# The first three loads of SyncE in another order, in a fused attention and feed-forward kernel

## Chip, cores and metric

The kernel runs on one core of a Trainium2 chip. The metric is the time of one execution in microseconds (us), measured on the device; the number given for a kernel is the median of its runs. The engines are named as in the profile: PE (TensorE matmuls), PEld (its weight loads), DVE (VectorE), ACT (ScalarE), POOL (GpSimd) and SP (SyncE), the last two of which here mainly issue DMAs.

## What is computed

Linear attention over 8 batches, 8 heads, 1024 positions and a head size of 64, followed by a feed-forward layer with a maximum of two branches. All inputs and outputs are float32.

```python
k_proj = einsum('ks,bhsd->bhkd', E, k)          # E: 64 x 1024
v_proj = einsum('ks,bhsd->bhkd', F, v)          # F: 64 x 1024
attn   = softmax(q @ k_proj^T / 8)              # over the 64 projected positions
x      = (attn @ v_proj), heads side by side    # 8192 x 512
out    = maximum(x @ w1, x @ w2) @ w_out        # 512 -> 1024 -> 512
```

## The kernel before, in words

Matmuls run in float16 with float32 sums. Loads of k, q, v and the weights go through POOL's DMA queue, which casts float32 to float16 on the way. The work is a list of steps by batch, written out by hand: each engine's instructions come in the order in which the program's steps are called. Batch 0 has a beginning of its own, which the change touches; from about 23 us on come the products of the feed-forward layer, with the attention of the next batch laid in between.

The beginning of batch 0, with the lines of the profile:

- SP issues three loads that aren't cast (L86 to L88): E into the first half of `ef_sb` (64 partitions of 4 KB, 256 KB), heads 0 and 1 of batch 0's k into `kf_sb` (128 partitions, two runs of 2 KB each, 512 KB), and F into the second half of `ef_sb` (256 KB). `ef_sb` lies in the buffer that the profile calls `big`; `kf_sb` uses the room of the later weight `wo_sb`.
- POOL issues, in its own queue (L108), heads 2 and 3 of k, heads 0 to 3 of q, 4 to 7 of k, 4 to 7 of q, then v in four loads of two heads each, then the weights (L130, L139, L143).
- DVE fills a tile with ones. PE runs eight matmuls on it (`warm(8)`, L153), whose results nobody reads; more such fillers stand between the later steps.
- `step_eft(0)`: PE turns E in eight float32 transposes (L167) and DVE casts the result to float16 (L173). `step_eft(1)` does so for F, with ACT casting.
- DVE casts head 0 of `kf_sb` (L959), ACT head 1 (L960).
- `warm(5)`, then `step_kv(t, 0, 4, "k")`: the product of E and heads 0 to 3 of k (L195). It needs the cast E, both casts of `kf_sb` and POOL's first load.
- `step_eft(1)`, then `step_kpt` (L285, L290) turns the projected k; `step_qt` (L311, L316) turns q; `step_sc` gives scores (L340) and exponentials on ACT (L380); `step_dn` the sums over the projected positions (L352) and their logarithm (L388); `step_inv` the reciprocal (L427). The same follows for heads 4 to 7.
- `step_kv(..., "v")` (L195) projects v with the turned F as its loads come in; `step_at` (L352, L443) forms the attention's output; the feed-forward products begin at L524.

The order on SP alone is what the change touches. Nothing in the program ties one of the three loads to another; what waits for them are the instructions that read their tiles: L167 for E and for F, L959 and L960 for `kf_sb`.

Of the kernel before, what the change touches and what calls it, by code (L numbers as in the profile page):

```python
# [19 lines left out]
def kernel(  # L20
# [12 lines left out]
    nc = tc.nc  # L33
# [5 lines left out]
    NC = S // 128  # L39
# [25 lines left out]
    def mm_bank(dtype=FP32, n=None):  # L65
        if n is None:
            n = turn.pop(0)
            turn.append(n)
        return ps.tile([128, 512 if dtype == FP32 else 1024], dtype, tag=f"mm{n}", name="mm_ps")
# [9 lines left out]
    def big(n, dtype=FP16):  # L79
# [3 lines left out]
    kf_sb = const.tile([128, 2048], FP32, tag="wo", name="kf_sb")[:, 0 : 2 * NC * D].rearrange(  # L83
        "p (h c d) -> p h c d", h=2, d=D
    )
    nc.sync.dma_start(out=ef_sb[:, 0, :], in_=E)  # L86
    nc.sync.dma_start(out=kf_sb, in_=k[0, 0:2].rearrange("h (p c) d -> p h c d", c=NC))
    nc.sync.dma_start(out=ef_sb[:, 1, :], in_=F)  # L88
    nc.scalar.add_instruction(
        mybir.InstLoadActFuncSet(  # L90
# [37 lines left out]
    for g in range(2):  # L128
        for w_sb, w in ((w2_sb, moe_w2), (w1_sb, moe_w1)):
            nc.gpsimd.dma_start(  # L130
                out=w_sb.rearrange("p (g z) f -> p g z f", z=2)[:, g, :, 0:256],
                in_=w.rearrange("(g p z) f -> p g z f", p=128, z=2)[:, g, :, 0:256],
            )
    for w_sb, w, f0, f1 in (
# [3 lines left out]
        for z in range(2):  # L138
            nc.gpsimd.dma_start(  # L139
                out=w_sb.rearrange("p (g z) f -> p g z f", z=2)[:, :, z, f0:f1],  # L140
                in_=w.rearrange("(g p z) f -> p g z f", p=128, z=2)[:, :, z, f0:f1],
# [994 lines left out]
    for i, (new, old) in enumerate(zip([*groups[1:], none], groups)):  # L1136
        n, h = divmod(i + 2, 2)
# [54 lines left out]
    for reg in regs:  # L1192
# [4 lines left out]
        out=mm_bank()[0:1, 0:1], lhsT=ones16[:, 0:1], rhs=ones16[:, 0:1], start=True, stop=True  # L1197
# [166 lines left out]
```

## Time and profile before

| | us |
|---|---|
| median of 3 runs | 319.77 (319.64 to 320.38) |
| the profiled execution | 319.9 |
| its span in the profile | 318.1 |
| PE busy in the span | 312.3 (98%) |
| DVE, ACT, POOL busy | 241.1, 206.2, 40.8 |

And the loads of the beginning, as the trace has them: when the issue began on its queue, how long it held it, and when the last of the 16 increments of the load's semaphore came (landing).

| load | queue | issue, us | held, us | landed, us |
|---|---|---|---|---|
| E | SP | 0.76 | 0.61 | 4.52 |
| k heads 2, 3 | POOL | 1.26 | 0.83 | 7.12 |
| k heads 0, 1 (`kf_sb`) | SP | 1.43 | 0.57 | 6.52 |
| F | SP | 2.04 | 0.50 | 8.16 |
| q heads 0 to 3 | POOL | 2.63 | 0.77 | 10.31 |
| k heads 4 to 7 | POOL | 3.39 | 0.75 | 12.82 |
| q heads 4 to 7 | POOL | 4.12 | 0.76 | 15.37 |
| v heads 0, 1 | POOL | 4.86 | 0.73 | 17.98 |
| v heads 2, 3 | POOL | 5.54 | 0.74 | 18.88 |

The profile's page gives busy time by engine; a busy PE is not a PE at its peak, and matmuls' ends are modelled. The timeline lists instructions by start, merged where they follow each other; in brackets stands the idle time of the engine just before and what ended it. The chain of waits is followed back from the last instruction, at each step to what released it. In the view of DMA, q1 is the queue that SP's loads take and q0 that of POOL's.

### The profile page before, as it was taken

To read this page: it belongs to the slowest core of one execution; us is meant where nothing else is said; L and a number is where in the kernel's file an instruction comes from. 1 tells how busy PE (TensorE), PEld (TensorE's weight loads), DVE (VectorE), ACT (ScalarE), POOL (GpSimd) and SP (SyncE) were. 2 spreads that over 40 slices of the span, in tenths; PEclk is the share of its full clock that TensorE was granted. 3 is DMA by queue.
4 is the path that set the end of the run, shared out by engine and by line. 5 is a ranking of instruction groups with operands and counts; after the bars stand their busy time and mean duration, and the time that the engine had idled before them with its cause. 6 is when DMAs were issued, how large, how long until landed. Compare 5 with 4: busy or idle time off the path is not lost.

```text
span 318.1 us, 9308 instructions
## 1 busy us (share of the span) xinstructions
PE 312.3 (98%) x3922; PEld 253.6 (80%) x3922; DVE 241.1 (76%) x441; ACT 206.2 (65%) x373; POOL 40.8 (13%) x63
## 2 busy tenths in 40 slices
PE   8989999999999999999999999999999999999996
PEld 3555588888887888788887888788887888888885
DVE  2366888877969696996969696996969696969883
ACT  2476842777776777477776778477776777765541
POOL 8259002003000300022000400030000000000000
PEclk9999999999999999999999999999999999999999
DMA  7999999999979999899999999989979131313124
GB/s 189 206 200 195 207 206 202 207 158 160 204 139 195 162 212 245 210 182 154 223 233 217 167 204 245 215 151 183 232 149 209 45 102 36 102 35 102 36 99 136
DMA packets 76684, 53.71 MB, mean 169 GB/s; under 512 B 29664, under 2 KB 76128, under 8 KB 76640
## 3 DMA queue, kind: packets, MB, share of 16 engines
q0 software_dynamic: 30688, 28.05, 56.0%
q1 hardware_dynamic: 45664, 24.85, 32.7%
q8 instruction: 31, 0.51, 0.6%
q10 hardware_dynamic: 288, 0.20, 0.2%
q14 instruction: 13, 0.11, 0.1%
HBM read 57.15 MB, written 16.78 MB: 232 GB/s over the span
## 4 chain that ended last, share of the span: by engine, by line
PE 92%; DMA 5%; POOL 1%; ACT 1%; issue 0%; DVE 0%; POOLq 0%
PE mm_ps L837 47%; PE mm_ps L745 27%; PE mm_ps L524 4%; DMA v_sb<-in_v_dram 4%; PE att_ps L352 3%; PE mm_ps L195 3%; PE mm_ps L340 2%; PE mm_ps L633 2%; PE att_ps L237 1%; DMA out_dram<-o_sb 1%; PE mm_ps L311 1%; POOL k_sb L108 0%; POOL q_sb L108 0%; ACT ld_sb L388 0%; ACT ex_sb L380 0%
## 5 line engine op out<-in xcount | busy, mean ns | idle before, releaser
L719 ACT COPY p_sb<-mm_ps 128x512 f32<-128x512 f32 x179 | 101.8, 592 | 49.1 <-PE mm_ps L745 27.2
L837 PEld LDWEIGHTS <-big 128*128 128x128 f16 x768 | 73.5, 98 | 11.8 <-issue 3.6
L837 PE MATMUL mm_ps<-T_sb,big 128*128 128x256 f16 x576 | 76.9, 273 | 0.0
L760 DVE TENSOR_TENSOR gt_sb<-mm_ps,p_sb 128x512 f16<-128x512 f32 x56 | 38.5, 687 | 43.0 <-PE mm_ps L745 41.6
L745 PE MATMUL mm_ps<-big,big 128*128 128x256 f16 x336 | 50.4, 273 | 0.0
L745 PEld LDWEIGHTS <-big 128*128 128x128 f16 x448 | 43.8, 98 | 5.1
L837 PE MATMUL mm_ps<-wo_sb,gt_sb 128*128 128x256 f16 x256 | 42.6, 273 | 0.0
L837 PEld LDWEIGHTS <-gt_sb 128*128 128x128 f16 x376 | 35.7, 98 | 6.7 <-issue 2.7
L469 ACT ACTIVATE ex_sb<-mm_ps 128x512 f16<-128x512 f32 x50 | 27.2, 596 | 18.0 <-PE mm_ps L340 12.3
L745 PEld LDWEIGHTS <-wd_sb 128*128 128x128 f16 x336 | 32.9, 98 | 3.8
L745 PE MATMUL mm_ps<-xt_sb,wd_sb 128*128 128x256 f16 x224 | 32.8, 273 | 0.0
L499 DVE TENSOR_TENSOR xt_sb<-att_ps,ld_sb 128x1024 f16<-128x1024 f32 x26 | 31.7, 1219 | 0.2
L837 PE MATMUL mm_ps<-m_sb,xt_sb 128*128 128x256 f16 x128 | 24.4, 273 | 0.0
L303 POOL COPY junk<-qt_sb 1x1 f16<-1x1 f16 x6 | 2.1, 346 | 172.5 <-DMA qt_sb<-q_sb 172.5
L868 DVE TENSOR_TENSOR o_sb<-mm_ps,p_sb 128x512 f32<-128x512 f32 x32 | 21.9, 683 | 2.8 <-ACT p_sb L897 2.0
L763 DVE TENSOR_SCALAR gt_sb<-gt_sb 128x512 f16<-128x512 f16 (+1 forms) x60 | 20.9, 348 | 2.1
L705 DVE TENSOR_TENSOR big<-gt_sb 128x1024 f16<-128x1024 f16 x32 | 21.8, 683 | 0.0
L837 PE MATMUL mm_ps<-wo_sb,big 128*128 128x256 f16 x128 | 21.5, 273 | 0.0
L806 ACT ACTIVATE gt_sb<-mm_ps 128x512 f16<-128x512 f32 x28 | 16.8, 601 | 5.7 <-PE mm_ps L745 5.7
L837 PE MATMUL mm_ps<-T_sb,gt_sb 128*128 128x256 f16 x120 | 20.3, 273 | 0.0
L837 PEld LDWEIGHTS <-xt_sb 128*128 128x128 f16 x188 | 18.3, 98 | 2.3 <-issue 0.2
L760 DVE TENSOR_TENSOR gt_sb<-p_sb 128x512 f16<-128x512 f32 x28 | 19.1, 682 | 0.6 <-ACT p_sb L719 0.6
(121 smaller groups left out, 434.7 us busy)
## 6 DMA issues: line engine op xcount, KB each, us to landing
out_dram<-o_sb SPq DMA_DIRECT2D x62, 256.0 KB
k_sb<-in_k_dram POOLq DMA_DIRECT2D x7, 1024.0 KB, 9.8
v_sb<-in_v_dram POOLq DMA_DIRECT2D x7, 1024.0 KB, 15.3
q_sb<-in_q_dram POOLq DMA_DIRECT2D x5, 1024.0 KB, 23.0
q_sb<-in_q_dram POOLq DMA_DIRECT2D x6, 512.0 KB, 15.8
big<-in_moe_w_dram POOLq DMA_DIRECT2D x12, 128.0 KB, 6.3
v_sb<-in_v_dram POOLq DMA_DIRECT2D x4, 256.0 KB, 13.6
wo_sb<-in_moe_w_out_dram POOLq DMA_DIRECT2D x1, 1024.0 KB, 10.4
```

What stands on the lines that cost most here:

```text
L195: nc.tensor.matmul(out=kv_ps[r * KP : (r + 1) * KP, h * D : (h + nh) * D], lhsT=eft[i][:, c, :], rhs=t[w][:, h0 + h : h0 + h + nh, c, :], ...
L469: nc.scalar.activation(out=t["ex", g, j][:, e, :], in_=banks[e], func=ACTF.Exp, scale=scale)
L499: nc.vector.tensor_tensor(out=x_out(t, g, j).rearrange("q z o n -> q o z n"), in0=at_ps.rearrange("q o (z n) -> q o z n", z=2), in1=ld[:, ...
L524: nc.tensor.matmul(out=h_ps, lhsT=wd_sb[:, r, fb * 128 : (fb + 1) * 128], rhs=t["xt"][:, r, :, j * W : (j + 1) * W], start=(r == 0), stop= ...
L705: nc.vector.tensor_tensor(out=S(i), in0=S(0) if x is None else x, in1=y(), op=op)
L719: copy(out=x, in_=bank)
L745: nc.tensor.matmul(out=bank[:, m * W : (m + 1) * W], lhsT=w_[:, n_, (2 * d + m) * 128 : (2 * d + m + 1) * 128], rhs=a[:, n_, :], start=(n ...
L760: nc.vector.tensor_tensor(out=c_blk(j, c), in0=two(x), in1=two(y), op=ALU.add)
L763: nc.vector.tensor_scalar_max(ap, ap, 0.0)
L806: nc.scalar.activation(out=out, in_=in_, func=ACTF.Relu)
L837: nc.tensor.matmul(out=bank[i][:, 0:CH] if two_banks else bank[:, i * CH : (i + 1) * CH], lhsT=a(c)[:, i * 128 : (i + 1) * 128], rhs=w_(c) ...
L868: nc.vector.tensor_tensor(out=o_sb, in0=two(x), in1=two(y), op=ALU.add)
```

## The change

SP issues the two heads of k first, then E, then F. Before it was E, the heads of k, F. Nothing else differs; every other engine has the same instructions in the same order.

```diff
     kf_sb = const.tile([128, 2048], FP32, tag="wo", name="kf_sb")[:, 0 : 2 * NC * D].rearrange(
         "p (h c d) -> p h c d", h=2, d=D
     )
+    nc.sync.dma_start(out=kf_sb, in_=k[0, 0:2].rearrange("h (p c) d -> p h c d", c=NC))
     nc.sync.dma_start(out=ef_sb[:, 0, :], in_=E)
-    nc.sync.dma_start(out=kf_sb, in_=k[0, 0:2].rearrange("h (p c) d -> p h c d", c=NC))
     nc.sync.dma_start(out=ef_sb[:, 1, :], in_=F)
```

## Prediction

> **What bounds the kernel now.** I read the chain of waits first, cut to the start and in order of time (start us, length us, what):
>
> ```profile
> 4.88 0.66 POOL v_sb L108
> 5.54 13.33 DMA v_sb<-in_v_dram
> 18.88 0.04 issue
> 18.92 0.64 PE mm_ps L195 x16
> 19.56 0.28 PE att_ps L352 x8
> 19.84 0.02 issue
> 19.86 0.60 ACT ld_sb L388
> 20.46 0.91 ACT ex_sb L380
> ```
>
> Up to 18.88 us the chain is GpSimd's stream of loads. Heads 2 and 3 of v land there, and PE takes them at once. Next I read the waits of PE from 23.3 us to the end of the span. That view has one row, at the very end:
>
> ```profile
> PE mm_ps L1196 <- DMA out_dram<-o_sb: 1.2, 1, 1.2
> ```
>
> The gaps between PE's matmuls from 23.3 to 316 us are 0.09 to 0.10 us each, where the shape changes; none is a wait for a transfer. So whatever moves the moment at which PE begins its unbroken run (L524 at 23.32) moves the end by as much. A delay ahead of it costs only what is over the slack at the start. The third view is the timeline of the first 24 us (start, length, engine, line, what, count, idle before and its releaser):
>
> ```profile
> 4.99 1.09 PE L167 MATMUL mm_ps<-ident,big 64*128 64x64 f32 x8
> ...
> 6.02 1.25 PE L153 MATMUL mm_ps<-ones 128*128 128x512 f16 x5
> 6.12 0.69 DVE L173 CAST eft<-mm_ps 128x512 f16<-128x512 f32 x1 [3.18 <-PE mm_ps L167]
> 6.55 0.62 ACT L960 CAST k_sb<-kf_sb 128x512 f16<-128x512 f32 x1 [4.51 <-DMA kf_sb<-in_k_dram]
> 6.73 0.51 DVE L959 CAST k_sb<-kf_sb 128x512 f16<-128x512 f32 x1
> ...
> 7.29 1.06 PE L195 MATMUL mm_ps<-k_sb,eft 128*64 128x256 f16 x8
> ```
>
> E has landed before kf: PE turns it (L167) from 4.99, DVE casts it (L173), and only then, behind that on DVE, stands the cast of kf's head 0 (L959). E's path is the long one, kf's the short one. In the trace's records of landings E is complete at 4.52, kf at 6.52, F at 8.16, GpSimd's first load (k heads 2 and 3) at 7.12, its first q load at 10.31.
>
> **The change, part by part.** No instruction is added or removed; PE, DVE, ACT and POOL keep their order; only the two DMA issues L86 and L87 change places on SyncE. Each occupies the queue 0.57 to 0.61 us, before and after. F stays third: the same bytes are ahead of it. It is needed only after the k product, so in the new order it has over 1 us of room where it had 0.14 us.
>
> *kf, now first:* it lands earlier, at some 5 us instead of 6.52. That buys nothing: ACT's cast L960 would start earlier and wait for nobody, and DVE's cast L959 stays behind L173. Value 0.
>
> *E, now second:* its landing sets everything. From E's landing to the first k product: F's row shows 0.14 us from landing (8.16) to first transpose (8.30); 0.81 from the first to the last of eight starts; 0.31 to DVE's cast (5.82 to 6.12); 0.61 to L959; 0.56 to the product (6.73 to 7.29). Sum 2.43 us. So the product starts at E's landing + 2.43, and its delay is d = landing + 2.43 - 7.29 = landing - 4.86. (PE's own path, transposes and the five filling matmuls, gives 2.35.)
>
> *Slack that d has to use up first.* The first q transposes (L311) start at 10.36, bound by q landing at 10.31; PE was free for them at 10.00 + 0.22 = 10.21, so 0.14 us is absorbed. After that two legs lead to the sums of 19.49 (L352):
>
> ```profile
> 17.82 1.02 ACT L380 ACTIVATE ex_sb<-att_ps 128x1024 f16<-128x1024 f32 x1 [0.57 <-PE att_ps L340]
> 18.03 0.47 PEld L195 LDWEIGHTS <-eft 128*64 128x64 f16 x16 [0.56 <-DMA v_sb<-in_v_dram]
> 18.03 0.64 PE L195 MATMUL mm_ps<-v_sb,eft 128*64 128x128 f16 x16 [0.28 <-DMA v_sb<-in_v_dram]
> ...
> 18.92 0.64 PE L195 MATMUL mm_ps<-v_sb,eft 128*64 128x128 f16 x16 [0.25 <-DMA v_sb<-in_v_dram]
> ```
>
> On PE, the two products of v wait for their loads: start to start, 0.34 and 0.42 us more than the same steps without a wait take. On ACT, the exponential that the sums read ends at 18.84; where the sums do wait for it (21.37 to 21.42) they start 0.05 later, so this leg has 19.49 - 18.89 = 0.59 us. The smaller leg decides: slack 0.14 + 0.59 = 0.74 us (PE's leg 0.14 + 0.34 + 0.42 = 0.90). From 19.49 on every step to 23.32 waits for PE, ACT or DVE, and GpSimd's transfers are there in time, so nothing more is absorbed. **The shift of the end is therefore E's landing - 5.60 us, and never below 0.**
>
> *E's landing in the new order.* No row has E behind kf; the nearest is F behind kf. The view of DMA queues by microsecond shows how the three loads (q1) ran beside GpSimd's stream (q0): 0.20 MB in 2 to 3 us, 0.26 in 3 to 4, 0.27 in 4 to 5 for q1; q0 joins with 0.04 MB in 4 to 5 and has 0.18 MB in 5 to 6. F's first packet starts at 6.06, just when kf's last does (6.05), although most of kf had ended at 5.44.
> - Low end: only bytes count. E and kf are 0.79 MB; the three microseconds from 2 to 5 moved 0.77 MB in all, so the last packet ends near 5.1, and with kf's 0.38 us from last packet to landing E is there at 5.5. Shift 0.
> - High end: kf takes as long as before, 2.93 us from first to last packet start (3.12 to 6.05); begun at 2.16, where E's first packet was, it ends at 5.09, and E then takes its own 2.36 us (2.16 to 4.52): 7.45. Shift 1.85 us.
> - Value taken: in the new order kf has the queue alone till q0's first packet at 4.07. Its packets ran at 131 per us when undisturbed (64 from 3.51 to 4.00), so 256 of them from 2.16 end at about 4.1, with a tail as on E (0.3) at 4.4; then F's time from first packet to landing (2.11) or E's (2.36), mean 2.2: 6.6 us. I take it because F behind kf is the very pattern, and because E and kf together had their last packet at 6.14 before, which no order of the same bytes shortens much.
>
> Shift 6.6 - 5.6 = 1.0 us. The profiled execution took 319.9 us by the clock outside and 318.1 as its span, so it would be 320.9 and a span of 319.1. It lies 0.13 above the median of 319.77, so the median comes to **320.8 us**.
>
> [...]
>
> **Rivals.**
> 1. *Absorbed, not slower.* The place is the wait for v at 18.03 and 18.92. If E's 64 large packets run through without F's gap and push q0 aside (as F's did: q0 fell from 0.18 MB in 5 to 6 us to 0.06 in 6 to 7), E lands at or below 5.6 and PE still reaches the sums by 19.49. The deciding point is 5.60 us; the time is 319.8, and up to 320.2 for a landing at 6.0. For: the low end above. Against: F's gap behind kf. Chance 0.18.
> 2. *The clock.* The first eight filling matmuls (L153, 1.47 to 5.06) start 0.43 us apart, the next five (from 6.02) 0.22 apart: PE's pace doubled close to 5 us, after 3.6 us without a break. In the new order PE runs dry from 5.06 to about 6.7. If the doubling has not come by then, eight transposes (0.11 us each) and five fillers (0.22) take twice as long, up to 0.9 + 1.1 = 2.0 us; I take half, as it can come in between: 321.8. For: the break falls at the turn itself. Against: the first two transposes, at 4.99 and 5.16, already run at nearly the fast pace. Chance 0.20. [...]
> 3. *Faster.* The stream of v lands a little earlier, as E and kf meet less of q0. At best PE reaches the sums 0.59 us earlier, since the exponential ends at 18.84, and only if E cost nothing: 319.2. Chance 0.07.
>
> **How the numbers follow.** Forecast (320.3 to 321.4) 0.55; rivals 0.18, 0.20, 0.07. The range 319.8 to 322.0 leaves out rival 3, part of the slow half of rival 2 and little else, under 0.2. What can be told from no change is 0.3%, or 0.96 us: slower means above 320.73, faster below 318.81. Just over half of the forecast and rival 2 lie above: 0.52; faster 0.03; the same 0.45.
>
> **What would show it.** In the profile after: ACT's L960 starts at 5 to 5.5 instead of 6.55 and still ends no wait of PE. PE has a hole between the fillers (5.06) and the transposes L167, which start near 6.7, released by E's load. L195's first group starts near 9.0. The waits for v at 18.03 and 18.92 are gone or shrunk; the sums wait for ACT's exponential; L524 begins at about 24.3; from there on the rows are as before, 1.0 us later. It is wrong if L167 starts below 5.8 (rival 1), if the fillers behind it are 0.43 us apart (rival 2), or if, after L524, waits of PE absorb the shift.

## The result, and the profile after

The changed kernel takes 321.62 us (median of 22 executions, 320.05 to 324.42) against 320.02 (22 executions, 319.59 to 320.68): 1.6 us more, a ratio of 1.0066 with a 95% interval of 1.0045 to 1.0087. Ratios here and below are not those of the medians (321.62 over 320.02 is 1.0050), and an execution more than 1.5% above the fastest of its kernel is left out of them. The forecast was 320.8, so the sign was right, and the rise of 1.6 us is over half as large again as the 1.0 us of the sum. The executions of the changed kernel scatter: four lie at 320.0 to 320.5, eleven at 321.0 to 322.6, seven at 323.6 to 324.4. The profiled one took 323.95 (span 322.2), so its rows show the effect at its largest, not at its median.

The chain of waits after, cut to the start (start us, length us, what):

```profile
1.27 5.17 DMA big<-in_E_dram
6.45 0.14 issue
6.58 1.12 PE mm_ps L167 x8
7.70 2.25 PE mm_ps L153 x5
9.95 1.84 PE mm_ps L195 x8
11.79 1.07 PE mm_ps L167 x8
12.86 0.35 PE mm_ps L285 x8
13.21 1.39 PE mm_ps L153 x3
14.61 1.71 PE mm_ps L311 x16
```

Where GpSimd's stream of v carried the chain up to 18.88, it is now E's load, and from 6.58 on PE. The timeline after (start, length, engine, line, what, count, idle before and its releaser) shows how:

```profile
4.26 0.62 ACT L960 CAST k_sb<-kf_sb 128x512 f16<-128x512 f32 x1 [2.22 <-DMA kf_sb<-in_k_dram]
...
6.58 1.12 PE L167 MATMUL mm_ps<-ident,big 64*128 64x64 f32 x8 [1.52 <-DMA big<-in_E_dram]
...
7.63 2.31 PE L153 MATMUL mm_ps<-ones 128*128 128x512 f16 x5
7.74 0.69 DVE L173 CAST eft<-mm_ps 128x512 f16<-128x512 f32 x1 [4.80 <-PE mm_ps L167]
8.35 0.42 DVE L959 CAST k_sb<-kf_sb 128x512 f16<-128x512 f32 x1
...
9.88 1.92 PE L195 MATMUL mm_ps<-k_sb,eft 128*64 128x256 f16 x8
```

Two things are to be seen. PE is dry for 1.52 us, until E has landed (6.45; before, 4.52). And PE then works at half its pace: five fillers in 2.31 us where it was 1.25, the k product in 1.92 where it was 1.06. The pace stays low until about 16.3 us: the clock's first record, at full clock, begins at 16.34 (before, at 5.52). The two v products no longer wait, and the sums wait for ACT's exponential, which was the leg named for the slack. First the scores and the sums of before, then the rows of after:

```profile
17.34 0.41 PE L340 MATMUL att_ps<-qt_sb,kpt_sb 64*32 64x256 f16 x16
...
19.49 0.30 PE L352 MATMUL att_ps<-ex_sb,ones 64*32 64x256 f16 x8
```

```profile
22.08 0.41 PE L340 MATMUL att_ps<-qt_sb,kpt_sb 64*32 64x256 f16 x16
...
22.56 1.02 ACT L380 ACTIVATE ex_sb<-att_ps 128x1024 f16<-128x1024 f32 x1 [0.57 <-PE att_ps L340]
...
23.64 0.30 PE L352 MATMUL att_ps<-ex_sb,ones 64*32 64x256 f16 x8
```

From the scores at 22.08 (before 17.34, 4.74 later) to these sums (19.49, 4.15 later) 0.59 us are absorbed. At the first feed-forward product (L524) the shift is still 4.15 us, and from 44 us to the end every matmul is 4.05 us later than before: almost nothing else gives any of it back.

### The profile page after: what moved, and what is told of

The parts are those of the page before. It is cut to its first block, busy times and chain, and to the rows that moved or that the text cites. A ratio compares the mean times of both kernels' runs of the same rounds, so it can differ in the third digit from the quotient of the medians.

```text
span 322.2 us, 9308 instructions
## 1 busy us (share of the span) xinstructions
PE 315.3 (98%) x3922; PEld 255.7 (79%) x3922; DVE 240.8 (75%) x441; ACT 206.0 (64%) x373; POOL 40.7 (13%) x63
## 4 chain that ended last, share of the span: by engine, by line
PE 95%; DMA 2%; ACT 1%; issue 0%; SPq 0%; DVE 0%
PE mm_ps L837 46%; PE mm_ps L745 27%; PE mm_ps L524 4%; PE mm_ps L195 4%; PE att_ps L352 3%; PE mm_ps L340 2%; PE mm_ps L153 2%; PE mm_ps L633 2%; DMA big<-in_E_dram 2%; PE mm_ps L311 1%; PE att_ps L237 1%; PE mm_ps L167 1%; DMA out_dram<-o_sb 1%; ACT ex_sb L380 1%; PE att_ps L340 1%; ACT ld_sb L388 0%
```

## The experiments

Theory C (clock): the hole in PE's work, between the last of the first fillers and E's landing, delays the doubling of PE's pace, by a piece that differs from execution to execution. Theory L (landing): only the later landings of E and of k's heads 2 and 3 cost time. Each ratio is against the kernel before, run in turn on the same chip.

| kernel | median us (lowest to highest) | before | ratio, 95% interval |
|---|---|---|---|
| changed, twelve fillers | 320.73 (320.14 to 323.66) | 319.98 | 1.0033 (1.0012 to 1.0053) |
| before, five fillers left out | 321.43 (320.38 to 323.92) | 319.98 | 1.0045 (1.0027 to 1.0063) |
| changed, sixteen fillers | 324.51 (322.14 to 325.72) | 319.98 | 1.0124 (1.0094 to 1.0155) |
| k first, E on ScalarE's queue | 321.19 (320.09 to 321.87) | 319.98 | 1.0028 (1.0015 to 1.0040) |
| before, twelve fillers | 320.32 (319.86 to 322.05) | 319.92 | 1.0018 (1.0007 to 1.0029) |
| changed, fourteen and three fillers | 321.24 (320.91 to 324.79) | 319.92 | 1.0039 (1.0026 to 1.0052) |
| before, three of the five fillers | 320.16 (319.85 to 322.06) | 319.92 | 1.0011 (1.0000 to 1.0022) |
| E on ScalarE's queue, ten fillers | 320.27 (320.03 to 321.93) | 319.92 | 1.0017 (1.0003 to 1.0031) |
| E, F, then k | 321.97 (320.42 to 325.62) | 319.99 | 1.0052 (1.0021 to 1.0084) |
| before, five transposes for the five fillers | 319.95 (319.51 to 322.61) | 320.04 | 1.0005 (0.9986 to 1.0024) |
| E, F on SyncE, k on ScalarE's queue | 321.98 (321.07 to 323.92) | 319.99 | 1.0071 (1.0050 to 1.0091) |

**Filling the hole.** In the changed kernel:

```diff
-    warm(8)
+    warm(12)
```

> The changed order with twelve filling matmuls at the start instead of eight, so that PE does not run dry between 5.06 and E's landing near 6.45. Theory C (the hole in PE's work delays the doubling of its pace): the five fillers after the transposes start 0.22 us apart instead of 0.43, and the median falls to 320.4 to 321.0 with no runs above 322. Theory L (only the later landings of E and of k's heads 2 and 3 count): the median stays at 321.6 and the spread of 4 us stays.

Measured: 320.73, 0.9 below the changed kernel, two of twelve executions above 322. The rows of its timeline, in an execution of 320.32 us:

```profile
6.08 1.09 PE L167 MATMUL mm_ps<-ident,big 64*128 64x64 f32 x8
7.11 1.25 PE L153 MATMUL mm_ps<-ones 128*128 128x512 f16 x5
...
8.29 1.06 PE L195 MATMUL mm_ps<-k_sb,eft 128*64 128x256 f16 x8
```

No wait stands before the transposes, and the five fillers take 1.25 us as before. C holds for the median and the pace; its "no runs above 322" does not. What stays, 0.75 us, is the order's own.

**A hole without a late load.** In the kernel before:

```diff
     nc.scalar.copy(out=t["k"][:, 1], in_=kf_sb[:, 1])
-    warm(5)
     step_kv(t, 0, 4, "k")
```

> The order of before, with the five fillers behind E's transposes left out: PE has a hole of some 1.3 us (5.9 to 7.2) but no load and no product is later. Theory C: the time rises by 1 us or more, with a spread of 2 us or more, and the fillers that remain are 0.43 us apart in some executions. Theory L: 320.0, within 0.2.

Measured: 321.43, with 320.38 to 323.92. The work left out has no use, the program moves no load, and the kernel is 1.45 us slower; C again. The view by stretches shows the clock (stretch, its length, busy us of PE, PEld, DVE, ACT and POOL, granted clock, DMA share, GB/s):

```profile
4.14:7.55 3.41, 1.60 (x11) 0.98 (x9) 1.33 (x2) 0.62 (x1) 3.41 (x5) 1.00 1.13 278
7.55:10.96 3.41, 3.12 (x24) 2.42 (x24) 0.42 (x1) 0.13 (x1) 1.22 (x3) 0.50 1.25 206
10.96:14.38 3.42, 3.42 (x28) 2.34 (x23) 1.08 (x3) 0.46 (x1) 1.03 (x2) 0.50 1.25 207
14.38:17.80 3.42, 3.42 (x62) 1.62 (x60) 1.01 (x2) 2.46 (x3) 1.41 (x2) 1.00 1.23 203
```

PE had the full clock at 4.14, was busy for 1.60 us of the next 3.41, and then ran 6.83 us at half clock, although it was busy for 6.54 of them. In this execution k's heads 2 and 3 landed at 7.71, so the hole was 1.97 us instead of 1.3 and the first k product 0.55 us later than before, less than the slack; its end was 2.0 us later.

**A small hole.** As above, with `warm(3)` in place of `warm(5)`.

> The order of before, with three instead of five fillers behind E's transposes: a hole of about 0.4 us before the first k product, no load or product later. [...] If any break in PE's work set the pace back, it would come out like the large hole, 321.4.

Measured: 320.16, 0.24 over before. The hole of 0.5 us there (0.52 in the trace) cost next to nothing in most executions. In the trace this break did not set the pace back: the k product behind it took 1.03 us (before, 1.06). One of the twelve, 322.06 us, had a mean granted clock of 0.989, so it did lose the pace; but so did one of the 17 executions of the kernel before in a later round (323.27 us, 0.989).

**The hole filled with transposes.** In the kernel before:

```diff
-    warm(5)
+    f_ps = mm_bank()
+    for _ in range(5):
+        nc.tensor.transpose(out=f_ps[:, 0:128], in_=ident, identity=ident)
     step_kv(t, 0, 4, "k")
```

> The order of before, with five float32 transposes of the 128 x 128 identity (their results unread) in place of the five fillers behind E's transposes: PE is busy for about as long, some 1.0 us, with as many instructions, but with transposes. If any busy time of PE counts for its clock, the time is before's, 319.9 to 320.2. If float32 transposes do not count, the stretch is a hole to the clock, and the time comes out like the kernel without the five fillers: 321 to 321.6, with executions up to 323 or more.

Measured: 319.95, the same as before, with two of twelve executions above 321. The transposes took 0.77 us and not 1.0, so a hole of 1 us stayed (0.98), and the time was kept in most executions. In the trace the k product behind it took 1.03 us, at the full pace, so these float32 transposes and the 0.98 us did not act as the hole of 1.97 us above did. Had they done so, it would have explained why the changed kernel stays slow so long; for E's and F's smaller ones (64 x 64) it was not tried.

**The delay without the hole and without the order.** In the kernel before:

```diff
-    warm(8)
+    warm(12)
```

> The order of before, with twelve fillers at the start instead of eight: E has landed at 4.5, but PE gets to its transposes only near 6.1, as late as in the changed order with twelve fillers. This is the delay of the data path alone, with PE's clock and the loads as before. By the sum of the prediction the shift is (start of the transposes - 0.14) - 5.60 = 0.3 to 0.4 us if the pace has doubled by 5.1: median 320.3 to 320.5, spread no wider than before's. If the start's slack were not 0.74 us but nothing, it would be 321.

Measured: 320.32, 0.4 over before. E has landed at 4.54, PE merely comes late to it. In the profiled execution the pace doubled only near 7.5 (the fillers are 0.43 us apart up to the transposes, and the five behind them take 1.25), so the transposes began at 6.70; the sum (6.70 - 0.14 - 5.60) gives 0.96, and that execution's span is 1.0 over before's. With twelve fillers in the changed order the transposes began at 6.08: the sum gives 0.34, and its matmuls at the end are 0.33 later. So the sum as a whole is right. Its parts are each a little off, and cancel: in both kernels the k product starts 2.35 us after the point that counts as E's landing (the sum had 2.43), and 0.66 us of its delay is absorbed (the sum had 0.74). One execution, 322.05 us, is further out than was expected.

**More cover.** In the changed kernel, sixteen fillers in place of eight; then fourteen, with `warm(3)` behind the transposes so that PE has as many instructions as with twelve and five.

> As the run with twelve fillers, but sixteen. Theory C: the pace doubles in every execution, spread under 1.5 us, and the median is 320.4 to 321.2 (the fillers themselves may end after E's landing and cost up to 0.5). Theory L: 321.6 or more.

> The changed order with fourteen fillers at the start and three instead of five behind E's transposes (as many instructions for PE as with twelve and five). Theory C: the hole is covered even when E lands near 6.4; no execution has the slow pace behind the transposes, median 320.4 to 320.9, and what stays over 321.3 comes from E landing late. Theory L: 321.6.

Both missed. Sixteen fillers: 324.51, no execution below 322. In the profiled one E landed only at 8.88, which puts the matmuls at the end 3.04 us later (the sum gives 3.3); and 2.7 us more come after the last matmul, where PE's last branch took 3.38 us instead of 0.39. The kernel has sixteen more instructions of PE (a weight load and a matmul for each filler); why the branch takes longer was not tried. So this kernel's time can't be read for C. Its trace speaks against a simple form of C: the pace doubled at 4.84, then came a hole of 2.27 us, the longest of all, and the clock stayed full (mean granted clock of that execution 0.998). Fourteen: 321.24. At half pace fourteen fillers end at 1.47 + 14 x 0.43 = 7.5, past E's landing, so the cover itself may come last; the five executions at 320.9 to 321.4, for which this would be the reason, have no trace. In the profiled execution, of 324.79 us, one of the 16 increments of E's landing came at 8.33, the other 15 by 5.60:

```profile
4.00 3.34 PE L153 MATMUL mm_ps<-ones 128*128 128x512 f16 x8
...
8.47 1.06 PE L167 MATMUL mm_ps<-ident,big 64*128 64x64 f32 x8 [1.13 <-DMA big<-in_E_dram]
...
10.65 1.92 PE L195 MATMUL mm_ps<-k_sb,eft 128*64 128x256 f16 x8 [0.36 <-DVE k_sb L959]
```

Here the pace had doubled at 6.9 and was lost again behind the hole: the granted clock was 0.50 from 10.33 to 17.16.

**E beside k, on a queue of its own.** In the changed kernel:

```diff
-    nc.sync.dma_start(out=ef_sb[:, 0, :], in_=E)
+    nc.scalar.dma_start(out=ef_sb[:, 0, :], in_=E)
```

> k's heads first on SyncE, but E issued at the same time from ScalarE's queue, so that E shares the transfer engines with k's heads instead of waiting behind them. Theory L: E lands near 5.0 to 5.6, the hole all but goes, and the median is 320.0 to 320.4. Theory C gives the same if the hole is under 0.3 us, and up to 321 if E lands past 5.6. If k's heads being first cost something by themselves, it would stay near 321.6.

Measured: 321.19, in two groups, 320.1 to 320.6 and 321.2 to 321.9. Issued at 0.76, as early as k's heads, E still landed at 5.78, since its first packet came at 3.58, when k's heads were nearly through (their last packet started at 3.92). The landing is just past the expected 5.6, and the time past what either theory gave. Then the same with `warm(10)` at the start:

> E on ScalarE's queue beside k's heads on SyncE, with ten fillers at the start, which close most of the hole of 0.85 us that E on ScalarE's queue left. Theory C: the upper cluster of that kernel (321.2 to 321.9) goes and the median falls from 321.2 to 320.2 to 320.5. Theory L: 321.2 again, since the loads are the same.

Measured: 320.27. The same loads with a shorter hole lose 0.9 us; nine of twelve executions are now below 320.8, but the upper group has not gone: three lie at 321.2 to 321.9. In the median that is C again, with other loads.

**Other orders.** E, F, then k's heads on SyncE; and E and F on SyncE with k's heads on ScalarE's queue.

> E, then F, then k's heads: E as early as before, k's heads behind F. Each load then lands by what stands ahead of it: k's heads near 7.5 to 8.0 (before 6.5), their casts end 0.7 later, the first k product starts near 8.3 to 8.7 instead of 7.29. By the sum with 0.74 us of slack the shift is 0.3 to 0.7. [...] Theory L: 320.3 to 320.7, narrow.

> E and F on SyncE, k's heads at the same time on ScalarE's queue. In the kernel with E on ScalarE's queue the load on SyncE was served first and E waited till it was through. If so here, E lands at 4.5, the rest as before: 319.9, and no hole. If the two share the transfer engines evenly, E lands near 5.5 and the time is 320.1 to 321 as with E on ScalarE's queue.

k third: 321.97, 320.42 to 325.62. Five executions lie at 320.4 to 320.8, which is the sum's part, with a mean granted clock of 0.998 to 1.000; the other seven, up to 325.6, have 0.983 to 0.995 and so lost the pace: in the profiled one k's heads landed at 9.15, PE was dry for 1.86 us, and the granted clock was 0.50 from 10.87 to 17.69. So k's heads come late third as E comes late second. k on ScalarE's queue was expected to be like before and was like the change: 321.98. ScalarE held the issue for 0.42 us and SyncE for 0.61, and k's heads went first, whole; E's first packet came at 3.41 and E landed at 5.68. A queue of its own did not let E share. In both kernels with two queues k's heads went first, once from SyncE and once from ScalarE, and both times their issue was the shorter one (0.46 us against 0.56 in the first, 0.42 against 0.61); which of the two decides is not shown.

None of these is faster than the kernel before.

## Why the prediction was too low

- *The end follows PE's start.* Right. After 27.5 us PE waits for a transfer once, at the very end, and from 44 us on the shift stays the same to 0.02 us, in the changed kernel as in the first four experiments.
- *k's heads first buy nothing.* Right: they landed at 4.24 instead of 6.52, ACT's cast began 2.3 us earlier, and no step of PE was earlier for it.
- *E's landing at 6.6.* Right in the profiled execution, 6.45; with twelve fillers 5.92, with fourteen 8.33, with sixteen 8.88. So the forecast's high end, 7.45, was passed in two of four traces of this order, and 6.6 was partly luck. How much of the spread of the times comes from late landings is not shown, as each kernel has one trace. The gap that F had behind k was not there: E's first packet started at 3.39, and some of its packets then took up to 1.15 us. Why, these runs don't show; GpSimd's stream starts in the same microseconds (0.08 MB from 4 to 5).
- *2.43 us from E to the k product, slack 0.74.* Right as a difference, by the two kernels with twelve fillers (2.35 and 0.66). For 6.45 the sum gives 0.85 us, and the median with the hole filled is 0.75 over before.
- *What the sum left out:* k's heads 2 and 3, GpSimd's first load, landed at 9.18 instead of 7.12. The sum charged GpSimd's queue nothing. At full pace the product would have waited for it, 0.4 us past E's path; in the profiled execution the slow fillers hid it.
- *The step that failed is the clock.* The forecast kept PE at full pace and left the clock to rival 2, with a chance of 0.20 and half of 2.0 us. It was the common case: 18 of 22 executions lie above 321, and with the hole filled 4 of 12. Filling the hole takes 0.9 of the 1.6 us away, and a hole alone, in the old order, adds 1.45. The profiled execution shows the sign that the prediction had named for rival 2: the fillers behind the transposes are 0.43 us apart. The price was low too: the slow stretch did not end with the fillers but went on for some 10 us (to 16.3), through the k product, the transposes of F and q and their fillers; in the profiled execution it is 4.05 - 0.85 = 3.2 us, 0.4 of which the late load of k's heads 2 and 3 would have cost at full pace too. The argument against it, that the transposes at 4.99 already ran fast, was no argument: the changed kernel's take 0.81 us from first start to last (6.58 to 7.39) at half pace, as F's did at full pace, so their spacing tells nothing of the clock. The clock's own records put the doubling at 5.5 us in the execution of before, and at 4.1 to 9.4 in those of the experiments; a hole from 5.06 on is ahead of it in many. Rival 2's other price, 0.9 us for the transposes, was for the same reason nothing.

The traces give no length of a hole at which the clock is lost: it was lost with the hole of 1.97 us in the old order and with that of 1.13 us with fourteen fillers, and kept with those of 0.98 us behind the transposes and of 2.27 us with sixteen fillers. In the kernel with the large hole the full clock lasted 3.41 us (4.14 to 7.55), of which PE was busy for 1.60, and the half clock behind it 6.83 us. The busy share doesn't tell the cases apart either: in the first 3.41 us after the doubling PE was busy for 1.56 us with k third and for 2.24 with fourteen fillers, and lost the clock, but for 1.91 with sixteen fillers, and kept it.

## What to carry to other kernels

Order the first loads by the length of the work behind each, not by size or by whose consumer looks busy: here E's path to the first product is 2.4 us long and that of k's heads 0.8 (6.52 to 7.29). In this case a late load at the start was charged twice, once for the delay that is over the slack (0.75 us in the median, with the hole filled) and once for PE's clock (0.9 us), when the hole fell ahead of the doubling (16.34 us in the changed kernel's trace) or, in some executions, soon behind it (k third: full clock from 7.45, half from 10.87). Before pricing such a hole look at the spread of executions, not at one profile, and test it by filling the hole and by making one where no data are late.

## What the runs showed that was not expected

- PE was busy for 9.7 us without a break (6.58 to 16.3) and stayed at half pace. The view by stretches of the changed kernel:

```profile
6.10:9.50 3.40, 2.92 (x13) 1.53 (x13) 1.02 (x2) 0.00 (x0) 1.63 (x4) 1.00 1.16 196
9.50:12.90 3.40, 3.40 (x22) 2.31 (x22) 0.42 (x1) 0.00 (x1) 1.38 (x2) 1.00 1.24 201
```

  PE is busy from 6.6 on, yet the pace doubles only near 16.3. (The clock column says 1.00 because the trace has no record of the clock before the doubling at 16.34; the fillers, 0.40 to 0.43 us apart up to 9.3 and at 13.2 to 14.0, show half pace.) In the kernel without the five fillers a stretch with 2.63 us of 3.40 busy (0.70 to 4.10) stood ahead of the full clock at 4.14; here one with 3.40 of 3.40 busy (9.50 to 12.90) was followed by half pace. What sets the clock these runs don't show; PE's busy share in the profile alone doesn't order the two.
- Two loads issued at the same time from SyncE and ScalarE were hardly interleaved: in the two kernels k's heads moved 0.26 and 0.31 MB in the microsecond from 2 to 3 us, and E's first packet came at 3.58 and 3.41, 0.3 to 0.4 us before the last of k's heads started.
- In the kernel with eight more fillers at the start PE's last branch, at the other end of the program, took 3.0 us longer in the one trace; with four more it took 0.38 us, as before. The reason was not tried.
